# First batch's keys pooled for both partition halves at once, normalising shared between two engines, and another order of the start

## The chip, the cores and the metric

The kernel runs on one core of one Trainium2 chip. The time is device time of one execution in microseconds (us). A core has a matrix engine (PE, which takes its stationary operand by a weight load, PEld, and writes into PSUM), a vector engine (DVE), an activation engine (ACT), GpSimd (POOL) and a queue processor (SP). Each works through its own instructions in order and meets the others at semaphores. In this kernel POOL issues nearly all input loads, and SP issues the stores and DMA transposes.

## The reference

Attention with pooled keys and values, followed by a mixer of two small networks, over 8 batches of 8 heads, 576 rows and head width 64. All inputs and the output are fp32.

```python
k_p = k.reshape(B, H, 72, 8, D).mean(axis=3)          # 576 rows pooled by 8
v_p = v.reshape(B, H, 72, 8, D).mean(axis=3)
scores = q @ k_p.T / sqrt(D);  attn = softmax(scores) # 576 x 72 per head
x = (attn @ v_p) laid out as [B, 576, 512]
u = x + (relu(x.T @ w_tok1) @ w_tok2).T               # token mix: 576 -> 256 -> 576
out = u + relu(u @ w_ch1) @ w_ch2                     # channel mix: 512 -> 1536 -> 512
```

## The kernel before

Each batch has a main part of 512 rows, four interleaved groups of 128 called j = 0 to 3, and a tail of 64 rows. A unit (class `Unit`) handles two groups of one batch: unit a has groups 0 and 1, unit c groups 2 and 3, and `TailUnit` t the tail. Units of batch 1 are a1, c1, t1, and of batch 2 a2, c2, t2. The names below are those of the code.

Attention of a unit goes like this. `qT` (L367) turns q on PE, `copy_qT` (L374) brings it to SBUF. `S(i)` (L382) computes scores against `kbd`, the pooled keys of a head in block-diagonal form: a [128, heads, 2, 72] tile in which the partitions 0 to 63 hold the keys for the first group of rows and the partitions 64 to 127 hold the same keys again for the second. So every pooled head must be copied twice, to two partition halves. The score index i stands for heads 0-2, 3-5 (432 columns of scores) and 6-7 (288 columns). `shift(i)` (L391) takes the row maximum on DVE. It has two forms. The plain one subtracts the maximum on DVE (L398, L400), and `do_E` then needs one exponential on ACT (L416). The "biased" one only takes the negated maximum (L395), and `do_E` (L404) runs one ACT activation of 72 columns per head and group, with the maximum as its bias (L413). `PT` (L424) turns the probabilities on PE, `copy_PT` (L430) copies them, `AV` (L439 to L457) multiplies by the pooled values `vpx` and sums the probabilities, and `norm` (`norm_first`, L459) divides on DVE by a reciprocal and one multiply over all eight heads.

Batch 0's keys are pooled in two halves of four heads (`pool_half`, L299), since they are loaded in two halves: heads 0-3 by SP as fp32, cast on DVE, and heads 4-7 by POOL. The pooling is a product with a banded matrix `pool_m` on PE. It makes two PSUM tiles per half: even heads land in the partitions 0 to 63, odd heads in 64 to 127. `copy_half` (L314) copies each into `kbd`, two copies of 64 partitions x 144 columns per call, four calls in all.

The token mix takes steps (`A_step`, L636, one per row group and a last one for the tail), a relu (`act_A`, L652, on ACT for half 0 and DVE for half 1), the second product and residual (`u`, L655; `add_u`, L664, on ACT for odd j and DVE for even j), and turns the result (`turn_u`, `copy_uT`, L670 and L675) for the channel mix. The channel mix (`c_stream`, from L1004) has for batch 0 three column blocks in which it starts with half of the rows (L1049), then wide blocks (L1017), then the second product (L1033), which uses `wc2` in three parts.

The order of the instructions is the order in which the functions are called; no scheduler changes it. `begin` (L764) holds two lists written by hand. The first (L771 to L861) covers batch 0's attention and token mix and is emitted as it stands. The second, from L863, covers batch 1's attention and token mix and the first steps of batch 2. It is woven with batch 0's `c_stream` by `weave` (L29), which takes from the one or the other so that the shares of the costs (the first argument of `add`) advance together. `fill` (L727), `warm` and the counts given to `S` and `AV` (`keep_running`, L256) add matmuls on a zero tile `idle` whose result is not used. From batch 2 on the streams are built by other functions.

Loads are issued on POOL in the order of the calls before `begin` (L1082 to L1094): `load_w_tok` (L233: w1m, w1t, w2r), `load(1, ...)` (L117: k, q of batch 1), the three parts of `w_ch1` and `w_ch2` (L245, L250), and among them `clear_probs` (L222), one memset on POOL that zeroes the unused columns of the probability tiles, and `split_w_tok2` (L241), two POOL copies.

Of the kernel before, what the change touches and what calls it, by code (L numbers as in the profile page):

```python
# [48 lines left out]
def kernel(  # L49
# [249 lines left out]
    def pool_half(hf):  # L299

        km, kt = main_t[0][0], tail_t[0][0]
        kp = [ps.tile([P, 2, SP], FP32, name="pa") for _ in range(2)]
        for i in range(2):
            for j in range(NJ):
                for hl in range(2):
                    nc.tensor.matmul(out=kp[hl][hl * D:(hl + 1) * D, i, 0:SPM], lhsT=km[:, 4 * hf + 2 * i + hl, j, :],
                                     rhs=pool_m[:, 0:SPM], start=(j == 0), stop=(j == NJ - 1))
        for i in range(2):
            for hl in range(2):
                nc.tensor.matmul(out=kp[hl][hl * D:(hl + 1) * D, i, SPM:SP], lhsT=kt[:, 4 * hf + 2 * i + hl, :],  # L310
                                 rhs=pool_t[0][:, SPM:SP], start=True, stop=True)
        half_ps[hf] = kp

    def copy_half(hf, hl, copy):  # L314
        heads = kbd[0].rearrange("p (r t) e n -> p r t e n", t=2)[:, 2 * hf:2 * hf + 2]
        src = half_ps[hf][hl][hl * D:(hl + 1) * D]
        copy(out=heads[0:D, :, hl, 0, :], in_=src)
        copy(out=heads[D:P, :, hl, 1, :], in_=src)
# [40 lines left out]
    class Unit:  # L359
# [82 lines left out]
        def norm(self, e):  # L442
            norm_first(*self.ao[e])
# [15 lines left out]
    def norm_first(xo, rows, ao, sums):  # L459
        den = sm_pool.tile([P, H], FP32, name="den")  # L460
        nc.vector.reciprocal(out=den[rows], in_=sums[rows])
        nc.vector.tensor_tensor(out=xo[rows].rearrange("p (h d) -> p h d", d=D), in0=ao[rows],
                                in1=den[rows, :, None].broadcast_to([rows.stop - rows.start, H, D]), op=ALU.mult)
# [23 lines left out]
    class TailUnit:  # L487
# [39 lines left out]
        def shift(self):  # L527
            self.sh = []
            for s in self.sc:
                mx = sm_pool.tile([P, 8], FP32, name="mx")  # L530
                nc.vector.tensor_reduce(out=mx[:, 0:HP], in_=s, axis=AX.X, op=ALU.max)
                sh = sh_pool.tile([P, 6, SP], FP32, name="sh")
                nc.vector.tensor_tensor(out=sh[:, 0:HP], in0=s, in1=mx[:, 0:HP, None].broadcast_to([P, HP, SP]),
                                        op=ALU.subtract)
                self.sh.append(sh)

        def do_E(self):
            self.probs = prob_t[self.g % 2]
            for i, sh in enumerate(self.sh):
                nc.scalar.activation(out=self.probs[:, i, :, 0:SP], in_=sh[:, 0:HP], func=AF.Exp)  # L540
# [48 lines left out]
        def norm(self):  # L589
            norm_first(*self.ao)  # L590
# [173 lines left out]
    def begin():  # L764
# [6 lines left out]
        add(0, fill, 11)  # L771
        add(0, fill, 16)
        add(0, pool_half, 0)
        add(0, c.qT, 0, HP)
        add(0, copy_half, 0, 1, nc.scalar.copy)
        add(0, pool_half, 1)
        add(0, copy_half, 0, 0, nc.scalar.copy)
        add(0, a.qT, 0, HP)
        add(0, c.qT, HP, H)
        add(0, c.copy_qT, 0, HP, nc.scalar.copy)  # L780
        add(0, a.qT, HP, H)
        add(0, a.copy_qT, 0, HP, nc.vector.tensor_copy)
        add(0, c.S, 0, 1)
        add(0, copy_half, 1, 1, nc.vector.tensor_copy)
        add(0, a.S, 0)
        add(0, c.shift, 0, True)
        add(0, copy_half, 1, 0, nc.scalar.copy)
        add(0, a.shift, 0, True)
        add(0, c.copy_qT, HP, H, nc.vector.tensor_copy)
        add(0, a.copy_qT, HP, H, nc.scalar.copy)  # L790
        add(0, a.S, 1, 1)
        add(0, a.S, 2, 1)
        add(0, c.do_E, 0)
        add(0, warm, 7)
        add(0, a.shift, 1, True)
        add(0, t.turn_q)
        add(0, c.S, 2)
        add(0, a.shift, 2, False)
        add(0, a.do_E, 0)
        add(0, c.shift, 2, False)  # L800
        add(0, c.S, 1, 1)
        add(0, a.do_E, 2)
        add(0, t.copy_qT)
        add(0, pool_v, 0)
        add(0, a.do_E, 1)
        add(0, a.PT, 0)
        add(0, a.PT, 1)
        add(0, c.do_E, 2)
        add(0, c.shift, 1, False)
        add(0, copy_v, 0)  # L810
        add(0, a.copy_PT, 0, nc.vector.tensor_copy)
        add(0, c.do_E, 1)
        add(0, t.S)
        add(0, a.copy_PT, 1, nc.scalar.copy)
        add(0, a.AV, 0, 1)
        add(0, t.shift)
        add(0, a.norm, 0)
        add(0, t.do_E)
        add(0, c.PT, 0)
        add(0, c.copy_PT, 0, nc.scalar.copy)  # L820
        add(0, a.AV, 1, 1)
        add(0, c.PT, 1)
        add(0, a.norm, 1)
        add(0, c.AV, 0, 1)
        add(0, t.PT)
        add(0, c.norm, 0)
        add(0, c.copy_PT, 1, nc.scalar.copy)
        add(0, c.AV, 1, 1)
        add(0, t.copy_PT, nc.scalar.copy)
        add(0, m0.A_step, (0,))  # L830
        add(0, t.AV)
        add(0, c.norm, 1)
        add(0, m0.A_step, (1,))
        add(0, m0.A_step, (3,))
        add(0, t.norm)
        add(0, m0.A_step, (2,))
        add(0, m0.A_step, (4,))
        add(0, m0.act_A, 0)
        add(0, m0.act_A, 1)
        add(0, a1.qT)  # L840
        add(900, a1.copy_qT, 0, H, nc.scalar.copy)
        add(0, m0.u, 2)
        add(0, m0.add_u, 2)
        add(0, m0.u, 1)
        add(0, m0.u, 0)
        add(0, m0.u, 3)
        add(0, m0.add_u, 1)
        add(0, m0.add_u, 0)
        add(0, m0.turn_u, 1)
        add(0, m0.turn_u, 0)  # L850
        add(0, sum_k, 1)
        add(0, m0.turn_u, 2)
        add(0, m0.add_u, 3)
        add(0, m0.copy_uT, 2, nc.scalar.copy)
        add(0, m0.copy_uT, 1, nc.vector.tensor_copy)
        add(0, m0.copy_uT, 0, nc.vector.tensor_copy)
        add(0, m0.turn_u, 3)
        add(0, m0.copy_uT, 3, nc.scalar.copy)
        add(0, copy_k, 1, 0)
        add(1170, copy_k, 1, 1)  # L860
        weave(Stream(), st)  # L861
        a2, c2, t2 = units(2)
        st = Stream()  # L863
        add = adder(st)
        add(0, a1.S, 0)
        add(0, c1.qT)
        add(0, t1.turn_q)
        add(0, load, 3, (2,))
        add(848, a1.shift, 0)
        add(0, a1.S, 1)  # L870
        add(1170, c1.copy_qT, 0, H, nc.vector.tensor_copy)
        add(0, c1.S, 0)
        add(0, a1.S, 2)
        add(530, a1.shift, 1)
        add(0, a1.do_E, 1)
        add(212, a1.shift, 2)
        add(1060, c1.shift, 0)
        add(0, c1.S, 1)
        add(1378, c1.shift, 1)
        add(0, a1.do_E, 0)  # L880
        add(0, c1.S, 2)
        add(0, a1.do_E, 2)
        add(0, pool_v, 1)
        add(0, a1.PT, 0)
        add(0, c1.do_E, 0)
        add(212, c1.shift, 2)
        add(1800, t1.copy_qT)
        add(0, c1.do_E, 1)
        add(0, t1.S)
        add(910, a1.copy_PT, 0, nc.vector.tensor_copy)  # L890
        add(0, c1.do_E, 2)
        add(0, load_v, 3, 0, 2)
        add(0, sum_v, 2)
        add(1060, t1.shift)
        add(540, copy_v, 1)
        add(0, c1.PT, 0)
        add(0, t1.do_E)
        add(0, a1.PT, 1)
        add(560, a1.copy_PT, 1, nc.scalar.copy)
        add(1400, c1.copy_PT, 0, nc.vector.tensor_copy)  # L900
        add(0, c1.PT, 1)
        add(1150, a1.do_AV, 0)
        add(0, t1.PT)
        add(1400, t1.copy_PT, nc.vector.tensor_copy)
        add(1150, t1.do_AV)
        add(910, c1.copy_PT, 1, nc.scalar.copy)
        add(1150, c1.do_AV, 0)
        add(0, c2.qT)
        add(920, c1.do_AV, 1)
        add(0, sum_k, 2)  # L910
        add(0, t2.turn_q)
# [225 lines left out]
```

## Time and profile before

| what | us or share |
|---|---|
| three timed runs | 279.21, 279.45, 279.54 (median 279.45) |
| the profiled execution | 279.35, of which the span from first to last instruction is 277.3 |
| PE busy | 269.7 (97%), 2174 matmuls |
| DVE, ACT, POOL busy | 164.0 (59%), 121.6 (44%), 116.2 (42%) |
| mean granted PE clock | 0.998 |
| DMA | 42.27 MB, mean 152 GB/s; q0, the loads that POOL issues, 17.93 MB |

A line of the timeline gives the start in the span, the time from the start of the first to the end of the last of a run of equal instructions, the engine, the source line, the operation, output<-inputs, shapes and count. In square brackets stands the idle time of that engine just before, and what ended it. A later instruction of an engine can start before the earlier one's recorded end, so costs in a row are taken from start to start. In a DMA issue line the last number is the time from issue to landing.

### The profile page before, as it was taken

The page shows a single profiled execution, that of the slowest core. Times are in us where ns is not written, and L with a number is a line of the kernel's source. Part 1 is how long each engine was busy: PE and PEld are TensorE (multiplying, and loading weights), DVE is VectorE, ACT ScalarE, POOL GpSimd, SP SyncE. Part 2 cuts the span into 40 slices and gives each one's busy share as a digit, 9 for nine tenths or more (in the row PEclk, how much of TensorE's full clock was granted, in tenths as well). Part 3 has the DMA queues.
Part 4 walks back from the last instruction along what each step waited for, and adds up shares of the span by engine and source line. Part 5 has one row for each costly group of instructions (what it writes and reads, how often), then busy time and mean ns, then how long its engine had stood idle before and what let it go on. Part 6 is the DMA issues. An engine that isn't in the chain of part 4 may idle for free.

```text
span 277.3 us, 5510 instructions
## 1 busy us (share of the span) xinstructions
PE 269.7 (97%) x2174; PEld 145.2 (52%) x2174; DVE 164.0 (59%) x379; ACT 121.6 (44%) x237; POOL 116.2 (42%) x159
## 2 busy tenths in 40 slices
PE   6799999999999999999999999999999999999994
PEld 4565856554445454474545544475544454554463
DVE  6386686688659852694479662775479452520112
ACT  6595587415533463045534552054623550036220
POOL 8699234785529868183459264920000000000000
PEclk9999999999999999999999999999999999999999
DMA  8999999996999999989997999658366701461013
GB/s 141 183 195 203 200 199 200 194 209 145 200 136 188 214 274 158 215 149 162 168 193 155 209 197 193 156 143 137 82 84 156 178 2 39 113 97 38 38 40 113
DMA packets 98969, 42.27 MB, mean 152 GB/s; under 512 B 68800, under 2 KB 94400, under 8 KB 98944
## 3 DMA queue, kind: packets, MB, share of 16 engines
q0 software_dynamic: 35616, 17.93, 49.6%
q1 hardware_dynamic: 63184, 23.93, 41.8%
q8 instruction: 17, 0.28, 0.4%
q10 hardware_dynamic: 144, 0.07, 0.1%
q14 instruction: 8, 0.07, 0.1%
HBM read 35.85 MB, written 9.44 MB: 163 GB/s over the span
## 4 chain that ended last, share of the span: by engine, by line
PE 90%; DVE 3%; DMA 2%; ACT 2%; POOL 1%; issue 1%; POOLq 0%
PE pa L1033 34%; PE pa L1017 31%; PE pa L682 4%; PE pa L478 3%; PE pa L388 3%; DMA qm<-in_q_dram 2%; PE pa L607 2%; PE pt L428 1%; ACT probs L413 1%; PE pa L661 1%; PE pa L625 1%; PE pt L625 1%; DVE xm L483 1%; PE pa L1049 1%; PE pt L372 1%; PE pa L645 1%
## 5 line engine op out<-in xcount | busy, mean ns | idle before, releaser
L1033 PE MATMUL pa<-wc,GT 128*128 128x512 bf16 (+2 forms) x444 | 104.1, 374 | 0.0
L1017 PE MATMUL pa<-uTm,wc 128*128 128x512 bf16 x372 | 89.6, 379 | 0.0
L1019 ACT ACTIVATE GT<-pa 128x512 bf16<-128x512 f32 x105 | 62.1, 597 | 62.5 <-PE pa L1017 62.2
L1017 PEld LDWEIGHTS <-wc 128*128 128x128 bf16 x564 | 44.8, 97 | 36.2 <-issue 1.2
L1033 PEld LDWEIGHTS <-GT 128*128 128x128 bf16 x444 | 41.0, 98 | 42.1 <-issue 1.2
L416 ACT ACTIVATE probs<-sh 128x432 bf16<-128x432 f32 (+1 forms) x45 | 22.9, 524 | 56.8 <-DVE sh L400 56.8
L1037 DVE TENSOR_TENSOR o<-pa,um 128x512 f32<-128x512 f32 (+2 forms) x33 | 22.1, 671 | 28.2 <-PE pa L1033 28.0
L355 POOL TENSOR_TENSOR s<-vs 72x512 f32<-72x512 bf16 x24 | 27.6, 1149 | 15.8 <-DMA vs<-in_v_dram 14.3
L400 DVE TENSOR_TENSOR sh<-pa,mx 128x432 f32<-128x432 f32 (+1 forms) x45 | 24.9, 554 | 3.8
L398 DVE TENSOR_REDUCE mx<-pa 128x6 f32<-128x432 f32 (+1 forms) x45 | 24.6, 546 | 3.2 <-PE pa L388 3.0
L483 DVE TENSOR_TENSOR xm<-pa,den 128x256 bf16<-128x256 f32 x56 | 23.8, 424 | 1.9
L482 DVE RECIPROCAL den<-pa 128x4 f32<-128x4 f32 x60 | 10.6, 177 | 18.6 <-PE pa L478 18.4
L1065 POOL DMA_DIRECT2D out_dram<-o x1 | 0.6, 620 | 49.2 <-DVE o L1037 49.2
L683 DVE TENSOR_TENSOR um<-pa,xm 128x512 bf16<-128x512 f32 x24 | 16.1, 688 | 5.6 <-PE pa L682 5.4
L356 POOL TENSOR_TENSOR s<-s 72x256 f32<-72x256 f32 x24 | 17.3, 722 | 1.9
L388 PE MATMUL pa<-kbd,qT 128*128 128x144 bf16 x128 | 15.4, 226 | 0.5 <-ACT qT L376 0.5
L388 PEld LDWEIGHTS <-qT 128*128 128x128 bf16 x128 | 10.7, 98 | 9.2 <-ACT qT L376 1.1
L478 PEld LDWEIGHTS <-pT 72*128 72x128 bf16 (+1 forms) x256 | 11.5, 99 | 6.8 <-issue 0.8
L682 PE MATMUL pa<-AT,w2m 128*128 128x512 bf16 x48 | 13.8, 379 | 0.0
L478 PE MATMUL pa<-vpx,pT 72*128 72x65 bf16 (+1 forms) x256 | 12.8, 194 | 0.0
L259 PE MATMUL pa<-idle 128*128 128x288 bf16 (+2 forms) x42 | 10.2, 389 | 2.2 <-DVE idle L168 2.2
L603 DVE TENSOR_SCALAR AT<-pa 128x512 bf16<-128x512 f32 x6 | 4.2, 692 | 13.1 <-PE pa L611 7.3
(150 smaller groups left out, 284.7 us busy)
## 6 DMA issues: line engine op xcount, KB each, us to landing
out_dram<-o SPq DMA_DIRECT2D x30, 256.0 KB, 2.5
vs<-in_v_dram POOLq DMA_DIRECT2D x7, 512.0 KB, 10.8
km<-in_k_dram POOLq DMA_DIRECT2D x7, 512.0 KB, 9.3
qm<-in_q_dram POOLq DMA_DIRECT2D x7, 512.0 KB, 12.1
wc<-in_moe_w_ch_dram POOLq DMA_DIRECT2D x6, 512.0 KB, 11.8
out_dram<-o SPq DMA_DIRECT2D x8, 128.0 KB, 2.4
o<-in_k_dram SPq DMA_DIRECT2D x2, 256.0 KB, 2.9
qm<-in_q_dram POOLq DMA_DIRECT2D x2, 256.0 KB, 6.1
```

The lines of the kernel that those rows point to most:

```text
L355: nc.gpsimd.tensor_tensor(out=s4, in0=vs[:, hs, 0:4], in1=vs[:, hs, 4:8], op=add)
L388: nc.tensor.matmul(out=sc[:, (h - h0) * 2:(h - h0) * 2 + 2, :], lhsT=qTs[self.b][:, 2 * h + self.jj, :], rhs=kbd[self.b % NB][:, h], start ...
L398: nc.vector.tensor_reduce(out=mx[:, 0:n], in_=sc, axis=AX.X, op=ALU.max)
L400: nc.vector.tensor_tensor(out=sh[:, 0:n], in0=sc, in1=mx[:, 0:n, None].broadcast_to([P, n, SP]), op=ALU.subtract)
L416: nc.scalar.activation(out=self.probs[:, :, h0:h1, 0:SP].rearrange("p e h n -> p h e n"), in_=self.sh[i][:, 0:(h1 - h0) * 2].rearrange("p ...
L478: nc.tensor.matmul(out=ao[r, hh, :], lhsT=probs_of(h, r), rhs=vpx[b % NB][:, h, :], start=True, stop=True)
L483: nc.vector.tensor_tensor(out=xo[rows, hf * HP * D:(hf + 1) * HP * D].rearrange("p (h d) -> p h d", d=D), in0=ao[rows, :, 0:D], in1=den[ro ...
L682: nc.tensor.matmul(out=u_ps, lhsT=w2m[:, m, j, :], rhs=ATs[b][:, m, :], start=(m == 0), stop=(m == 1))
L1017: nc.tensor.matmul(out=g_ps[:, i, :], lhsT=wc1[:, kk, m * P:(m + 1) * P], rhs=uTs(kk, 0, width), start=(kk == 0), stop=(kk == 3))
L1019: nc.scalar.activation(out=GT[:, m0:m0 + per, :], in_=g_ps, func=AF.Relu)
L1033: nc.tensor.matmul(out=hold["ps"], lhsT=GT[:, kk, j * P:(j + 1) * P], rhs=wc2[:, kk, cols], start=(kk == 0), stop=(kk == NM - 1))
L1037: nc.vector.tensor_tensor(out=o_sb, in0=hold["ps"], in1=us(j)[:, cols], op=ALU.add)
```

## The change

`pool_half` makes one PSUM tile per half with all four heads and computes each head twice, into the partitions 0 to 63 and 64 to 127: 40 matmuls for 20. `copy_half` is then one copy of 64 partitions x 288 columns (all four heads) per call, with the partition half as its argument. There are four copies in all for eight; DVE does those of the upper partition half, ACT those of the lower.

`norm` takes a flag `shared`: DVE multiplies five heads, and ACT scales the other three with one activation of 64 columns each. Only c's second group uses it. The tail unit's `shift` and `do_E` get the biased form. Which groups are biased changes: before, c's 0 and a's 0 and 1; after, c's 0 and 2 and the tail.

The first list is reordered: a's scores start before q's second half is turned for c, c's second q copy goes to ACT, a's second pT copy goes from ACT to DVE, the tail's `AV` goes ahead of the second `A_step`, and 22 fillers stand ahead of the pooling for 27. The second list has another order and other weights. On POOL, `clear_probs` goes ahead of all of these loads, and the third part of `w_ch1`, batch 1's v and `split_w_tok2` change places with others.

```diff
     def pool_half(hf):
 
         km, kt = main_t[0][0], tail_t[0][0]
-        kp = [ps.tile([P, 2, SP], FP32, name="pa") for _ in range(2)]
-        for i in range(2):
+        kp = ps.tile([P, HP, SP], FP32, name="pa")
+        for i in range(HP):
             for j in range(NJ):
-                for hl in range(2):
-                    nc.tensor.matmul(out=kp[hl][hl * D:(hl + 1) * D, i, 0:SPM], lhsT=km[:, 4 * hf + 2 * i + hl, j, :],
-                                     rhs=pool_m[:, 0:SPM], start=(j == 0), stop=(j == NJ - 1))
...
+                for rows in half:
+                    nc.tensor.matmul(out=kp[rows, i, 0:SPM], lhsT=km[:, HP * hf + i, j, :], rhs=pool_m[:, 0:SPM],
+                                     start=(j == 0), stop=(j == NJ - 1))
...
-    def copy_half(hf, hl, copy):
-        heads = kbd[0].rearrange("p (r t) e n -> p r t e n", t=2)[:, 2 * hf:2 * hf + 2]
-        src = half_ps[hf][hl][hl * D:(hl + 1) * D]
-        copy(out=heads[0:D, :, hl, 0, :], in_=src)
-        copy(out=heads[D:P, :, hl, 1, :], in_=src)
+    def copy_half(hf, e, copy):
+        rows = slice(e * D, (e + 1) * D)
+        copy(out=kbd[0][rows, HP * hf:HP * hf + HP, e, :], in_=half_ps[hf][rows])
...
+    def norm_first(xo, rows, ao, sums, shared=False):
         den = sm_pool.tile([P, H], FP32, name="den")
         nc.vector.reciprocal(out=den[rows], in_=sums[rows])
+        hv = H - 3 if shared else H
+        nc.vector.tensor_tensor(out=xo[rows, 0:hv * D].rearrange("p (h d) -> p h d", d=D), in0=ao[rows, 0:hv],
+                                in1=den[rows, 0:hv, None].broadcast_to([rows.stop - rows.start, hv, D]), op=ALU.mult)
+        for h in range(hv, H):
+            nc.scalar.activation(out=xo[rows, h * D:(h + 1) * D], in_=ao[rows, h, :], func=AF.Copy,
+                                 scale=den[rows, h:h + 1])
...
     # TailUnit.shift(biased), TailUnit.do_E: as Unit's
+                if biased:
+                    nc.vector.tensor_reduce(out=mx[:, 0:HP], in_=s, axis=AX.X, op=ALU.max, negate=True)
+                    self.sh.append((s, mx))
+                    continue
...
+                    for h in range(HP):
+                        nc.scalar.activation(out=self.probs[:, i, h, 0:SP], in_=sh[0][:, h, :], func=AF.Exp,
+                                             bias=sh[1][:, h:h + 1])
```

The first list after the change, to the end of the attention:

```python
fill 16, fill 6, pool_half 0, copy_half(0, 1, DVE), a.qT(0, 4), c.qT(0, 4), c.copy_qT(0, 4, DVE),
copy_half(0, 0, ACT), pool_half 1, copy_half(1, 1, DVE), a.copy_qT(0, 4, ACT), a.S(0, 1 filler), a.qT(4, 8),
c.S(0, 1), copy_half(1, 0, ACT), a.copy_qT(4, 8, DVE), c.shift(0, biased), a.S(1, 1), c.qT(4, 8), a.shift(1),
warm 9, c.copy_qT(4, 8, ACT), c.do_E 0, a.shift(0), a.S 2, c.S(1, 1), a.do_E 0, t.turn_q, t.copy_qT, a.shift(2),
c.S(2, 1), a.do_E 1, pool_v, a.do_E 2, c.shift(2, biased), c.do_E 2, c.shift(1), a.PT 0, copy_v,
a.copy_PT(0, DVE), a.PT 1, t.S, a.AV 0, c.do_E 1, c.PT 0, t.shift(biased), a.copy_PT(1, DVE), t.do_E,
a.AV(1, 1), c.copy_PT(0, ACT), a.norm 0, c.PT 1, a.norm 1, c.copy_PT(1, ACT), t.PT, c.AV 0, A_step 0, c.norm 0,
c.AV 1, t.copy_PT, t.AV(1), A_step 2, A_step 1, c.norm(1, shared), t.norm, A_step 3, A_step 4
```

On POOL:

```diff
+    clear_probs()
     load_w_tok()
     load(1, (0, 1))
     load_w_ch1(0)
-    clear_probs()
+    load_w_ch1(2)
     load_w_ch1(1)
+    load(1, (2,))
+    split_w_tok2()
     load_w_ch2(0)
-    load(1, (2,))
-    load_w_ch1(2)
-    split_w_tok2()
     load_w_ch2(1)
     load(2, (1, 0, 2))
     load_w_ch2(2)
```

More of the change, by code (lines that the diff above doesn't have):

```diff
@@ L525, in S, with shift @@
             self.sc = sc
[L527 removed]
+        def shift(self, biased=False):
             self.sh = []
@@ L836, in begin @@
-        add(0, m0.A_step, (2,))
         add(0, m0.A_step, (4,))
-        add(0, m0.act_A, 0)
         add(0, m0.act_A, 1)
         add(0, a1.qT)
-        add(900, a1.copy_qT, 0, H, nc.scalar.copy)
+        add(0, m0.act_A, 0)
+        add(0, m0.u, 0)
+        add(0, m0.add_u, 0)
+        add(180, a1.copy_qT, 0, H, nc.scalar.copy)
         add(0, m0.u, 2)
-        add(0, m0.add_u, 2)
         add(0, m0.u, 1)
-        add(0, m0.u, 0)
         add(0, m0.u, 3)
         add(0, m0.add_u, 1)
-        add(0, m0.add_u, 0)
+        add(0, m0.turn_u, 0)
@@ L935, in begin @@
+        add(690, m1.add_u, 2)
+        add(0, m1.uT, 2, 2)
+        add(0, copy_k, 2, 0)
+        add(1800, t2.copy_qT)
         return st
```

217 lines of the change are left out of this document (107 added, 110 removed).

## The prediction

> **What bounds the kernel now.** I read the page's busy table and its chain of waits first, then the stretches before the steady part, then the timelines of ACT, DVE, PE and POOL and the DMA issues there.
>
> ```profile
> PE 269.7 (97%) x2174; PEld 145.2 (52%) x2174; DVE 164.0 (59%) x379; ACT 121.6 (44%) x237; POOL 116.2 (42%) x159
> ...
> PE 90%; DVE 3%; DMA 2%; ACT 2%; POOL 1%; issue 1%; POOLq 0%
> ```
>
> Over the whole span PE is the bound; the chain leaves it for a tenth. Where it leaves it is seen in a table of stretches (engine busy times, granted clock, DMA share, GB/s):
>
> ```profile
> 10.54:12.96 2.42, 1.88 (x21) 1.25 (x22) 1.69 (x5) 1.61 (x4) 0.93 (x1) 1.00 1.72 185
> 12.96:22.33 9.37, 9.16 (x139) 6.35 (x137) 8.15 (x18) 9.36 (x28) 8.89 (x8) 1.00 1.46 195
> 22.33:29.83 7.50, 7.48 (x103) 4.45 (x100) 5.02 (x11) 2.80 (x5) 5.67 (x9) 1.00 1.26 207
> 29.83:61.80 31.97, 31.97 (x312) 19.60 (x310) 23.99 (x56) 18.45 (x35) 17.81 (x25) 1.00 1.43 203
> ```
>
> From 29.83, where batch 0's channel mix begins (L1049), PE is busy 31.97 of 31.97: what arrives earlier there ends earlier, and what DVE or ACT do there is covered. From 12.96 to 22.33 ACT is busy 9.36 of 9.37: batch 0's exponentials and copies set that stretch. PE's 9.16 there are no bound, since they contain 7 fillers in a row and single ones (L259, matmuls whose result is not used). Before 10.54 the loads set the pace:
>
> ```profile
> 9.23 0.44 PE L306 MATMUL pa<-pool_m,km 128*64 128x64 bf16 x16 [0.56 <-DMA km<-in_k_dram]
> ...
> 10.54 0.62 PE L372 MATMUL pt<-ident,qm 128*128 128x128 bf16 x8 [0.50 <-DMA qm<-in_q_dram]
> ```
>
> So the change can act on three pieces: from 10.54 to ACT's first exponential, ACT's stretch, and the token mix to 29.83.
>
> **Pooling and its copies.** 40 matmuls a half for 20. The 16 L306 of a half begin at 9.23 and the next line at 9.50 follows: 0.27/16, about 0.017 each in pairs of column halves, so 20 more cost 0.31 or so. Half 0 runs before km's second half lands (9.15), half 1 before q's second half lands (10.54), and five fillers fewer (22 for 27; 27 take 5.75 from 2.17 on, 0.21 each) come ahead: nothing on the path. Without that cover it would be 2x0.31. The copies: eight at 0.27 to 0.31 become four of 64x288, whose rows exist at L333 (DVE 0.46, ACT 0.39-0.40). Both read one tile now, and ACT's waits for DVE's. The second half's pair is done near 11.0, when the first scores can start; before, the last of them was DVE's at 11.98+0.31.
>
> **To the first exponential.**
>
> ```profile
> 11.20 0.42 DVE L376 COPY qT<-pt 128x512 bf16<-128x512 bf16 x1 [4.69 <-PE pt L372]
> 11.65 0.31 DVE L317 CAST kbd<-pa 64x144 bf16<-64x144 f32 x1
> 11.98 0.31 DVE L318 CAST kbd<-pa 64x144 bf16<-64x144 f32 x1
> 12.32 1.12 DVE L395 TENSOR_REDUCE mx<-pa 128x6 f32<-128x432 f32 x2
> ```
>
> DVE does two small copies behind the last q copy and ahead of the first maximum. Both are gone from that place, and c's scores no longer need q's second half: its first maximum can start near 11.34, 0.98 earlier. ACT gains less, as c's second q copy now lies ahead of the exponentials: it starts near 11.99 (PE turns c's second half after a's and two score matmuls) and takes 0.48 to the next start. First exponential 12.47 for 12.96: -0.5.
>
> **ACT's stretch.**
>
> ```profile
> 12.96 2.64 ACT L413 ACTIVATE probs<-pa,mx 128x72 bf16<-128x72 f32 x12 [0.34 <-DVE mx L395]
> ...
> 15.99 1.48 ACT L413 ACTIVATE probs<-pa,mx 128x72 bf16<-128x72 f32 x6
> ...
> 19.81 1.92 ACT L431 COPY pT<-pt 72x1024 bf16<-72x1024 bf16 x2
> ```
>
> A biased group costs ACT an activation per head; from start to start 0.205 (15.99 to 17.22 for six). One unbiased activation of 432 columns takes 0.45 (18.03 to 18.48), one of 288 columns 0.33, but costs DVE a subtract (0.52 or 0.37). Before: 18x0.205 + 0.45 + 3x0.34 + vpx 0.48 + q-tail copy 0.25 + three pT copies (0.98, 0.92, 0.94) and the tail's 0.58 make 9.3, which is the stretch. After: biased are c0 (6), c2 (4), t (4), so 14x0.205; a0, a1, c1 unbiased 3x0.45; a2 0.33; 0.25; 0.48; two pT copies 1.8; 0.58. That is 7.66, or 1.64 less. Given back: DVE, which gets two subtracts of 432 and one pT copy (0.60) and loses two of 288, works through c0's maximum, a1, a0, a2, c2, c1 from 11.34 with no pause, so a0's subtract ends near 14.25 while ACT is through c0 at 13.70: 0.55 of waiting; t's maximum is late too, 0.2, and the last pT 0.2. ACT's last copy ends at 12.47+7.66+0.95, near 21.1, for 22.33: -1.2, of which -0.5 came in with the first exponential. If DVE's chain is as slow as its longest rows (0.60 for the reduce, 0.61 for the subtract: +0.09 each over four pairs) 0.5 is lost; if ACT never waits, 0.95 is gained.
>
> **Shared normalising.** c's second group: DVE's multiply goes from 512 columns (0.61) to 320 (about 0.42 in proportion); ACT does three of 64 columns. The nearest rows are L413's 72 columns, 0.205 each, so 0.6 on an ACT that has ended its copies. ACT ends after DVE by some 0.2 to 0.4, but x_tail's multiply, last before the token mix's tail step, comes 0.19 earlier. I take 0, with 0.2 either way. The new order of steps, tail last, then lets the token mix (PE 7.48 busy of 7.50) begin 1.2 earlier and keep all but 0.2 at its ACT and DVE hand-overs (idle PE is some tenths at 24.7 to 29.8, and act_A, add_u only change engine order): L1049 near 28.85 for 29.83, -1.0.
>
> **Batch 1 woven in.** The matmuls are the same ones in another order; PE has no gap there to fill and none to spare. A wait that the new order opens shows as a gap, a saved one as nothing: 0.1 either way for none seen, up to +0.3.
>
> **The moved memset and loads.** POOL issues the loads, and a memset stands between them:
>
> ```profile
> 7.88 0.60 POOL L236 DMA_DIRECT2D w1m<-in_moe_w_tok_dram  x1
> ...
> 13.44 0.69 POOL L142 DMA_DIRECT2D kt<-in_k_dram  x1 [1.73 <-DMA vs<-in_v_dram]
> ...
> 16.41 3.88 POOL L223 MEMSET probs<- 128x4480 bf16 x1
> ```
>
> Its 3.77 (16.41 to 20.18) now come at 7.88: w1m, both w1t, w2r, and batch 1's k issue from 11.65, 3.3 to 3.8 later. Against that, POOL waited 0.51 and 1.73 for landings before the old place, which the memset now fills, so q of batch 1 goes out 1.6 later and the second wc chunk 2 earlier. What matters is whether the DMA engines go empty. At 7.88 they have v and the q tail ahead of them, to 14.1 (issue 7.21 plus 6.9). A load of 512 KB, km at 161.2, landed after 6.7 on a quiet queue; at 200 GB/s 2.6 of that is transfer, so data begins some 4.1 after issue: 15.75 for a 256 KB w1m with half of that transfer still to come, at worst, where its landing was 15.3. I take a slip d of 0 to 0.45 for the stream. The slowest quiet row (vs at 72.47, 384 KB in 8.8) allows 4.5 for w1m's slip. The loads keep their total, so the last one of this phase to be late counts:
>
> ```profile
> wc<-in_moe_w_ch_dram POOLq DMA_DIRECT2D x1, 512.0 KB, 13.2
> ```
>
> This is w_ch2's third part, issued at 37.85, landed 51.05, first used by L1033 at 52.83: 1.78 of slack. With PE 1.0 earlier and d to 0.45 it still holds. Batch 1's q (issued 14.11, 9.1 to landing, needed at about 24) has 0.6. The new order of the w_ch1 chunks puts the one needed last in third place, at about 31.3 for a need after 33.
>
> A rule of the Trainium skill speaks against the moved memset: by its page "SBUF — State Buffer", section "Who interferes with whom", VectorE's second port pair is GpSimd's and is taken as an exclusive lock, and the loser waits. This is a rival below, priced there by rows.
>
> **Sum.** The profiled run took 279.35, span 277.3 and 2.05 around it, 0.1 under the median 279.45. First exponential -0.5, ACT's stretch -0.7, lost in the token mix +0.2, woven part and shared multiply 0, loads 0, rounded: -1.1 from 279.35 is 278.25, and with the median's 0.1, 278.3. Own range 277.8 to 278.8 (DVE's chain +0.5, ACT's waits -0.5).
>
> **Rivals.**
> 1. A late load gives the gain back. It decides from d over 0.6 (batch 1's q) or 0.7 (w_ch2's third part, 1.78-1.1). For it: w1m alone slips 3.8 at issue. Against: the two waits that absorb it, and PE can go on with channel mix. Half to all of the 1.1 is lost: 278.8 to 279.4.
> 2. The stream starves by the whole 3.77 of POOL. It decides from d over 1.78: 279.35+3.77-1.78 = 281.3. For it the 8.8 of vs; against it km's 6.7, and loads queued to 14.1.
> 3. The memset holds up DVE from 7.9 to 11.65, just where four copies and the first maximum now lie: if these wait to 11.65, two kbd copies (0.46), two q copies (0.33) put the maximum at 13.2, 0.9 after the old one: 279.45+0.8 = 280.3. Against it: pT's copy ran inside the old memset in 0.69 (17.71) and outside, at 39.37, in 0.68. The Trainium skill has the reason in "VectorE: DVE Perf Modes", section "Why PSUM operands drop a tier": an operand in PSUM never uses the second port; the trace agrees.
> 4. DVE is the bound of the stretch, nearly as long as ACT was: its 8.15 busy plus 2x0.52+0.60-2x0.37 is 9.05, less copies that come earlier. Then ACT's 1.64 counts for nothing, only the earlier maximum's 0.98 less 0.3: 278.8.
> 5. ACT hardly waits, 0.95 more: 277.4.
>
> **How the numbers follow.** Forecast with case 4's near end 0.63; case 1 0.20; case 5 0.08; case 2 0.06; case 3 0.03. No more than 0.2% (0.56) either way cannot be told from no change: all of 278.9 to 280.0. From case 1 most of 0.20 less 0.06, plus 0.02 of the rest: same 0.16; slower 0.09 from cases 2, 3; faster 0.75. Range 277.7 to 279.3: the low end half of case 5, the high end nearly all of case 1.
>
> **What would show it.** Right: the first L395 at 11.3, first L413 near 12.5, ACT's last pT copy near 21.1, first L1049 near 28.8, PE without gaps after. Wrong: 64x288 copies beyond 0.46 or ending after 11.2 (case 3); w1m landing beyond 17, or PE idle behind a DMA at 24, 33 or 52 (1, 2); DVE busy and ACT waiting over 1.5 from 12 to 21 (4); L1049 early but the end not, with PE gaps behind DVE or ACT between 30 and 62: the woven order.

## The result: slower, and the profile after

The changed kernel takes 283.76 us (median of four runs, 283.03 to 284.05) against 279.44 (279.21 to 279.54) for the kernel before: a ratio of 1.015, 95% interval 1.0129 to 1.0172. The prediction said 278.3. The profiled execution took 283.62, span 281.6, which is 4.3 more than the span before.

The page's busy table and chain of the changed kernel:

```profile
PE 267.7 (95%) x2182; PEld 146.6 (52%) x2210; DVE 169.5 (60%) x379; ACT 120.7 (43%) x232; POOL 116.1 (41%) x159
...
PE 85%; DVE 8%; DMA 2%; POOL 1%; issue 1%; ACT 1%; DVEq 0%; POOLq 0%
```

PE's busy time is 2.0 less than before, it covers 85% of the chain, not 90%, and DVE 8% where it had 3%. DVE's busy time is 5.5 more with the same 379 instructions, so some DVE instruction has become long. The table of stretches tells where PE stood (engine busy times in the order PE, PEld, DVE, ACT, POOL, then granted clock, DMA share, GB/s):

```profile
0.00:10.54 10.54, 4.88 (x54) 3.37 (x55) 8.30 (x17) 4.68 (x10) 9.34 (x18) 1.00 1.03 152
10.54:12.96 2.42, 1.11 (x16) 1.06 (x15) 1.88 (x3) 0.20 (x1) 2.42 (x4) 0.77 1.60 166
12.96:22.33 9.37, 9.23 (x127) 6.48 (x126) 7.44 (x16) 6.30 (x20) 7.39 (x10) 0.88 1.20 147
```

ACT has 0.20 of work from 10.54 to 12.96 where it had 1.61. Everything is late before ACT's stretch begins. The timeline of the changed kernel, POOL's line first, then DVE, PE, ACT and PE again:

```profile
7.88 3.88 POOL L223 MEMSET probs<- 128x4480 bf16 x1
...
5.71 6.28 DVE L189 COPY pool_t<-diag 64x8 bf16<-64x8 bf16 x2 [0.24 <-POOL diag L184]
...
11.85 0.33 PE L310 MATMUL pa<-pool_t,kt 128*64 128x8 bf16 x7 [4.79 <-DVE pool_t L189]
...
17.14 1.38 ACT L411 ACTIVATE probs<-pa,mx 128x72 bf16<-128x72 f32 x6
...
33.10 1.91 PE L1060 MATMUL pa<-uTm,wc 128*128 128x256 bf16 x16
...
75.92 0.43 PE L480 MATMUL pa<-vpx,pT 72*128 72x65 bf16 x8 [1.22 <-DMA pT<-probs]
```

And the same DVE line in the kernel before:

```profile
5.71 0.80 DVE L189 COPY pool_t<-diag 64x8 bf16<-64x8 bf16 x2 [0.24 <-POOL diag L184]
```

Two copies of 64x8 elements, which make the pooling matrix for the tails (`pool_t`, L186 to L190, in code that the change does not touch), went from 0.80 to 6.28 us together: the first took 6.08 for 0.16, the second 0.17 for 0.61. The first ends at 11.79, when POOL's memset ends (7.88 + 3.88 = 11.76). PE needs `pool_t` for the last matmuls of each pooled half (L310), so it stood for 4.79 behind 32 matmuls that were done. The first biased exponential comes at 17.14 for 12.96, the channel mix at 33.10 for 29.83: 3.27 later. The rest of the 4.3 is a second place, PE's wait of 1.22 at 75.92 for the transposed probabilities of batch 2; the kernel before has no wait over 0.2 after 17.32.

### The profile page after: what moved, and what is told of

Read it like the earlier page. It is cut to its first block, busy times and chain, and to the rows that moved or that the text cites. A ratio compares the mean times of both kernels' runs of the same rounds, so it can differ in the third digit from the quotient of the medians.

```text
span 281.6 us, 5553 instructions
## 1 busy us (share of the span) xinstructions
PE 267.7 (95%) x2182; PEld 146.6 (52%) x2210; DVE 169.5 (60%) x379; ACT 120.7 (43%) x232; POOL 116.1 (41%) x159
## 4 chain that ended last, share of the span: by engine, by line
PE 85%; DVE 8%; DMA 2%; POOL 1%; issue 1%; ACT 1%; DVEq 0%; POOLq 0%
PE pa L1044 31%; PE pa L1028 30%; PE pa L693 3%; PE pa L480 3%; PE pa L386 2%; DVE pool_t L189 2%; DVE sh L398 2%; PE pa L618 2%; DMA pT<-probs 2%; DVE mx L396 2%; PE pa L672 1%; PE pa L636 1%; PE pt L636 1%; PE pt L370 1%; PE pa L1060 1%
## 5 line engine op out<-in xcount | busy, mean ns | idle before, releaser
L1044 PE MATMUL pa<-wc,GT 128*128 128x512 bf16 (+2 forms) x426 | 101.7, 373 | 1.1 <-issue 0.3
L353 POOL TENSOR_TENSOR s<-vs 72x512 f32<-72x512 bf16 x24 | 27.6, 1149 | 14.8 <-DMA vs<-in_v_dram 13.4
L398 DVE TENSOR_TENSOR sh<-pa,mx 128x432 f32<-128x432 f32 (+1 forms) x46 | 25.7, 559 | 3.9
L396 DVE TENSOR_REDUCE mx<-pa 128x6 f32<-128x432 f32 (+1 forms) x46 | 25.3, 551 | 3.1 <-ACT GT L1063 1.5
L693 PE MATMUL pa<-AT,w2m 128*128 128x512 bf16 x45 | 13.1, 379 | 0.0
L267 POOL COPY kk<-km 128x1024 bf16<-128x1024 bf16 x8 | 8.1, 1036 | 10.9 <-DMA km<-in_k_dram 8.4
```

The costliest lines, as they stand in the source:

```text
L353: nc.gpsimd.tensor_tensor(out=s4, in0=vs[:, hs, 0:4], in1=vs[:, hs, 4:8], op=add)
L396: nc.vector.tensor_reduce(out=mx[:, 0:n], in_=sc, axis=AX.X, op=ALU.max)
L398: nc.vector.tensor_tensor(out=sh[:, 0:n], in0=sc, in1=mx[:, 0:n, None].broadcast_to([P, n, SP]), op=ALU.subtract)
L693: nc.tensor.matmul(out=u_ps, lhsT=w2m[:, m, j, :], rhs=ATs[b][:, m, :], start=(m == 0), stop=(m == 1))
L1044: nc.tensor.matmul(out=hold["ps"], lhsT=GT[:, kk, j * P:(j + 1) * P], rhs=wc2[:, kk, cols], start=(kk == 0), stop=(kk == NM - 1))
```

## The experiments

Fifteen kernels. "Ratio" is against the kernel before that was timed with it, with its 95% interval where there is one. "Start" is the first biased exponential, "mix" the first matmul of the channel mix, "wait" PE's wait for `pT` between 70 and 76, in the profiled execution as "start" and "mix" are.

| kernel | median, before beside it | ratio | start | mix | wait |
|---|---|---|---|---|---|
| before | 279.44 | | 12.96 | 29.83 | none |
| changed | 283.76 | 1.015 (1.0129 to 1.0172) | 17.14 | 33.10 | 1.22 |
| e1 memset in its old place | 278.81 / 279.23 | 0.9983 (0.9969 to 0.9998) | 12.43 | 28.90 | 1.30 |
| e2 before, memset first | 282.89 / 279.23 | 1.0129 (1.011 to 1.0149) | 16.47 | 33.36 | none |
| e3 pool_t copied by ACT | 281.13 / 279.23 | 1.007 (1.0049 to 1.0092) | 12.31 | 29.96 | 1.34 |
| e4 memset four issues later | 279.98 / 279.23 | 1.0024 (1.0008 to 1.0041) | 12.58 | 30.42 | none |
| e5 e1, old second list | 278.41 / 279.59 | 0.9949 (0.9929 to 0.9968) | 12.61 | 28.57 | none |
| e6 before, new pooling alone | 280.32 / 279.59 | 1.0026 (1.0014 to 1.0038) | 12.35 | 29.88 | 1.23 |
| e7 memset in four pieces | 283.31, one run | | 17.90 | 33.85 | none |
| e8 pool_t by tensor_tensor | 281.50, one run | | 12.91 | 30.11 | none |
| e9 memset one issue later | 284.56, one run | | 18.55 | 35.10 | none |
| e10 memset near 39 us | 278.85 / 279.36 | 0.9977 (0.9963 to 0.9991) | 12.98 | 28.94 | none |
| e11 e10, norm not shared | 278.71 / 279.36 | 0.9977 (0.9961 to 0.9993) | 12.20 | 28.74 | 1.44 |
| e12 before, 36 more matmuls | 280.18 / 279.36 | 1.0024 (1.0005 to 1.0042) | 13.13 | 30.02 | 1.25 |
| e13 memset three issues later | 280.47, one run | | 12.64 | 29.42 | none |
| e14 e10, 36 more matmuls | 278.17 / 279.23 | 0.9957 (0.994 to 0.9974) | 12.14 | 28.35 | none |
| e15 e10, old second list | 278.65 / 279.23 | 0.9977 (0.9959 to 0.9995) | 12.79 | 28.75 | none |

"Start" has to be read beside the landing of k's second half, which moves by some tenths from one execution to another: PE begins the second pooling at 9.23 in before, at 9.09 in e1, 9.28 in e5, 9.63 in e10, 8.76 in e14.

### Is it the memset, and what does it hold?

e1 puts the memset back in the changed kernel; e2 moves it, and nothing else, in the kernel before.

```diff
 e1, against the changed kernel            e2, against the kernel before
-    clear_probs()                         +    clear_probs()
     load_w_tok()                               load_w_tok()
     load(1, (0, 1))                            load(1, (0, 1))
     load_w_ch1(0)                              load_w_ch1(0)
+    clear_probs()                         -    clear_probs()
```

> The changed kernel with the POOL memset of the probability tiles put back behind w_ch1's first part, all else as changed. Theory L (the memset, recorded from 7.88 to 11.76, holds DVE's 64x8 copy of pool_t, which took 6.08 us instead of 0.61, and with it the pooling): the copy takes about 0.6 again, the first biased exponential starts near 12.5 instead of 17.14, the first matmul of the channel mix near 28.9 instead of 33.10. The end is then 278.3 if nothing else is wrong with the prediction, and about 279.4 if PE's 1.22 us wait at 75.92 for the turned probabilities of batch 2 belongs to the new second list (theory W) and stays. Rival P (the doubled pooling or the new copies cost the time): first exponential stays beyond 15, the end over 281.

> The kernel before, with only the memset moved ahead of the late loads. Theory L: DVE's copy of pool_t again takes about 6.1 us, PE waits nearly 5 us for it, the first exponential comes 4 to 5 us later than 12.96, and the end is 283 to 284. Rival P: the memset alone does little, the end is 279.2 to 280.

e1's first exponential is at 12.43 and its channel mix begins at 28.90; theory L holds and P falls. The time is 278.81, between the two that were named, and its ten runs form two groups, 277.98 to 278.49 and 279.13 to 279.47; the profiled one belongs to the upper. Its PE timeline:

```profile
24.64 0.39 PE L672 MATMUL pa<-AT,w2m 128*128 128x512 bf16 x1 [0.22 <-POOL w2m L243]
25.22 0.82 PE L672 MATMUL pa<-AT,w2m 128*128 128x512 bf16 x3 [0.19 <-POOL w2m L243]
...
71.81 0.43 PE L480 MATMUL pa<-vpx,pT 72*128 72x65 bf16 x8 [1.30 <-DMA pT<-probs]
```

PE is now early enough to wait for POOL's split of w_tok2, 0.41 in all, and in this execution the wait for `pT` takes the gain back. e2 is 3.66 us slower than before, with its first exponential 3.5 later (4 to 5 were expected), and its two copies again take 6.28 together, so the new pooling is not needed for the loss.

e3 lets ACT make `pool_t`, e8 keeps DVE but uses an addition of two SBUF tiles, e7 cuts the memset in four.

```diff
-        nc.vector.tensor_copy(out=pool_t[s][half[s], SPM:SP], in_=diag[...])
+        nc.scalar.copy(out=pool_t[s][half[s], SPM:SP], in_=diag[...])                   # e3
+        nc.vector.tensor_tensor(out=pool_t[s][half[s], SPM:SP],                         # e8
+                                in0=pool_t[s][half[s], SPM:SP], in1=diag[...], op=ALU.add)
...
-        nc.gpsimd.memset(prob_all.rearrange("p t e h n -> p (t e h) n")[:, :, SP:P], 0.0)
+        cols = prob_all.rearrange("p t e h n -> p (t e h) n")                           # e7
+        for c in range(SP, P, 14):
+            nc.gpsimd.memset(cols[:, :, c:c + 14], 0.0)
```

> The changed kernel, memset in front, with the two 64x8 copies of pool_t done by ACT instead of DVE, so that DVE has no copy from SBUF to SBUF left there. If the memset only holds DVE's operation between SBUF tiles (theory L, narrow): the two kbd copies of DVE run at about 0.46 inside the memset, the first exponential is near 12.5, the end 278.3 (279.4 with theory W). If it holds every DVE operation (theory L, wide): DVE's first kbd copy does not end before 11.7, the first exponential comes at 15 or later, the end over 281. If POOL's loads being 3.8 us later is what costs, the end stays over 280 with an early first exponential and PE waits on DMA.

> The changed kernel, memset in front, with DVE's two 64x8 copies of pool_t made as additions of diag to the zeroed tile (tensor_tensor with both inputs in SBUF). If every DVE operation between SBUF tiles is held by the memset, the first addition takes about 6 us and the end is 283.6. If it is the copy's form that is held, the additions take under 0.7 together and the end is that of e3, about 281.1. The Trainium skill (page SBUF - State Buffer, section Who interferes with whom) says the second: a DVE instruction with two SBUF inputs is held only by a GpSimd instruction that reads SBUF, and a memset only writes.

> The changed kernel, memset in front, made by four memsets of 14 columns each (about 0.97 us apiece) that follow each other. If DVE's copy of pool_t is held for one instruction of POOL at a time (L, each), it ends when the first piece ends, near 8.9 or earlier, and the end is that of e3, about 281.1. If it is held as long as POOL has such work without a break (L, whole), it ends near 11.8 as in the changed kernel, and the end is 283.6.

In e3 and e8 the memset still runs from 8.01 and 7.91 for 3.88, and inside it DVE copies `kbd` out of PSUM in 0.46, as outside. e8's two additions take 0.34 together:

```profile
5.73 0.34 DVE L189 TENSOR_TENSOR pool_t<-pool_t,diag 64x8 bf16<-64x8 bf16 x2 [0.25 <-POOL diag L184]
```

So neither DVE as such nor all its work between SBUF tiles is held, only the copy. This is what the Trainium skill says on its page "SBUF — State Buffer", section "Who interferes with whom": a copy between SBUF tiles can take the port pair that VectorE shares with GpSimd, and a two-input operation is held only by a GpSimd instruction that reads SBUF. The traces agree on who is held and who is not; the ports themselves are in no trace. In e7 the copy ends at 12.28, with the last of four memsets (8.26 + 4.00 = 12.26): it does not get in between them.

But e3 and e8 are not fast. e3's PE timeline and its row of the stretch that had 195 GB/s before:

```profile
25.62 0.62 PE L370 MATMUL pt<-ident,qm 128*128 128x128 bf16 x8 [1.92 <-DMA qm<-in_q_dram]
...
53.97 1.02 PE L1044 MATMUL pa<-wc,GT 128*128 128x512 bf16 x4 [1.02 <-DMA wc<-in_moe_w_ch_dram]
```

```profile
12.96:22.33 9.37, 8.91 (x151) 6.86 (x151) 8.41 (x20) 7.82 (x24) 7.52 (x10) 1.00 1.15 139
```

The loads are late. Batch 1's q, issued at 15.69, lands 9.9 later, at 25.6 for 23.2; w_ch2's third part lands at 53.9 (40.49 + 13.4) for 51.05. The stretch moved 56 GB/s less for 9.37 us (e1, with the memset in its old place, moved 196), that is 0.52 MB, which at 200 GB/s is an estimated 2.6 us of transfer. In the changed kernel none of this shows, since PE itself is over 3 us late.

### From where does the hold begin?

The copy started 2.17 ahead of the memset and yet lost to it. e4, e9 and e13 move the memset behind all four, one and three issues of `load_w_tok`.

> The changed kernel with the memset four DMA issues later, behind load_w_tok, at about 10.3 to 14.2. Theory L, narrow: the copy of pool_t takes about 0.6, DVE's copies and maxima out of PSUM run inside the memset at their usual times, the end within 0.4 of e1's. Theory L, wide: DVE stands from 10.3 to 14.2, the first exponential is near 16, the end over 281.

> The changed kernel with the memset one DMA issue later, behind w1m, at about 8.4 to 12.3. The copy of pool_t starts at 5.71, 2.2 us ahead of the memset's recorded start in the changed kernel, and was held all the same; with four issues between (e4) it was not. If the hold begins with the memset's own time on POOL and the copy merely failed to get in before it, one more issue of 0.55 us changes nothing: the copy takes over 6 us, PE waits 5 us for it, the end is 283.6. If POOL's next work decides when the copy is let in, it is free at about 6.3 as before, and the end is that of e3 and e8, 280.7 to 281.5.

> The changed kernel with the memset three DMA issues later, behind w2r, at about 9.7 to 13.6. In e9 (one later) the copy of pool_t, started at 5.71, was held 6.64 us, to 12.35; in e4 (four later) it was not held. If the hold reaches back a fixed time of some 2.7 us from the memset's start, the copy is free near 6.3 here. If it reaches back by instructions, it is free only from four on: held to 13.6, PE waits over 6 us, the end near 285.

The DVE and POOL timelines of e9:

```profile
5.71 6.84 DVE L189 COPY pool_t<-diag 64x8 bf16<-64x8 bf16 x2 [0.24 <-POOL diag L184]
```

```profile
8.44 3.89 POOL L223 MEMSET probs<- 128x4480 bf16 x1
```

and of e13:

```profile
5.71 0.80 DVE L189 COPY pool_t<-diag 64x8 bf16<-64x8 bf16 x2 [0.24 <-POOL diag L184]
```

```profile
9.68 3.90 POOL L223 MEMSET probs<- 128x4480 bf16 x1
```

A memset recorded 2.73 after the copy's start holds it, one recorded 3.97 after does not (nor e4's at 10.20). In before the first of the two copies is done at 5.87 (5.71 and 0.16), and up to there POOL's recorded instructions are the same in all these kernels, so the hold reaches back at least 2.0 us ahead of the memset's recorded start in the changed kernel and 2.6 in e9. In e13 the second copy is done 3.2 ahead of it. Whether what decides is a time between the two or a number of instructions in POOL's queue (the memset was the fourth and fifth behind `diag` where it held, the seventh and eighth where it did not) stays open. In e4 DVE's maxima and subtracts ran inside the memset at their usual 0.60 and 0.61; e4 and e13 lose by loads instead (PE waits 1.18 and 0.93 for batch 1's q, e13 another 0.95 for w_ch2), so e4 is not within 0.4 of e1, as theory L had it, but 1.2 above.

### The second wait, at 70 to 76

e5 and e15 use the second list as it was; e6 puts only `pool_half` and `copy_half` into the kernel before.

> The kernel of e1 (memset in its old place) with the second list of begin as it was before the change. Theory W (PE's wait of 1.30 us at 71.81 in e1 for batch 2's turned probabilities belongs to the new second list): no wait over 0.4 on PE between 60 and 80, the first channel-mix matmul at 28.9 as in e1, and this 0.9 is kept to the end: 278.3. Rival W2 (the wait comes with any list once PE starts 0.9 earlier, since the chain of batch 2 over DVE, ACT and SP does not): a wait of 0.9 or more stays, the end at 279.2, as before.

> The kernel before with only pool_half and copy_half as changed (40 matmuls a half, one copy of 64x288 per call), in the old order. If the four copies are what they cost elsewhere (DVE 0.46, ACT 0.39), the last kbd copy on DVE ends 0.1 to 0.2 earlier than 12.29, the first maximum and the first exponential with it, and the end is 0.1 to 0.3 lower: 279.0. If the doubled matmuls are on the path (theory P), the first exponential is 0.2 to 0.6 later than 12.96 and the end 279.5 to 279.9.

e5 came out as theory W had it, 278.41 and no wait. But e6, which has the old list, waits 1.23 at 72.79 (and at 280.32 ends above both of its forecasts), and e8, which has the new one, does not: W falls. What goes with the wait is a packet of instructions on the queue q8. Every trace has 17 of them:

```profile
q8 instruction: 17, 0.28, 0.4%
```

The sixth comes between 69 and 78 (in e14 near 63), and in every trace a hole in the transfers follows it. The half microseconds of before and of the changed kernel (last column GB/s; the packet is in 74.00 and in 73.00):

```profile
74.00:74.50 0.50, 0.41 (x2) 0.10 (x1) 0.47 (x2) 0.40 (x1) 0.50 (x1) 1.00 1.71 211
74.50:75.00 0.50, 0.44 (x3) 0.20 (x3) 0.01 (x1) 0.00 (x0) 0.50 (x2) 1.00 0.16 16
75.00:75.50 0.50, 0.50 (x4) 0.26 (x3) 0.00 (x0) 0.31 (x1) 0.50 (x2) 1.00 0.30 41
```

```profile
73.00:73.50 0.50, 0.50 (x5) 0.25 (x4) 0.47 (x3) 0.28 (x1) 0.00 (x0) 1.00 1.10 193
...
74.00:74.50 0.50, 0.50 (x4) 0.10 (x1) 0.49 (x2) 0.23 (x1) 0.00 (x0) 1.00 3.76 44
74.50:75.00 0.50, 0.20 (x1) 0.00 (x0) 0.43 (x3) 0.26 (x1) 0.00 (x0) 1.00 0.04 3
75.00:75.50 0.50, 0.00 (x0) 0.00 (x0) 0.37 (x2) 0.34 (x1) 0.00 (x0) 1.00 0.09 10
```

In before the last transpose of c2's probabilities had landed by then, and a later transpose of q takes the hole. In the changed kernel a transpose of c2's, issued at 70.88, lands in 5.0 where the same one took 3.3 in before (issued at 67.69), and PE goes empty. All 17 traces fit this. Where the sixth packet comes 2.4 to 3.1 us after that transpose is issued (changed, e1, e3, e6, e11, e12), the transpose lands in 5.0 to 5.2 and PE waits 1.22 to 1.44. Where it comes 3.8 us or more after (e2, e4, e5, e7 to e10, e13, e15 and before), or ahead of it (e14), it lands in 3.2 to 3.3 and PE does not wait. Up to the half microsecond of the packet PE had 729 weight loads in before and 729 in the changed kernel, 730 in e1 and e3, and 739 to 748 in e5, e6, e8 and e10, so it seems to come by PE's place in its own instructions. The change adds 36 matmuls (2210 weight loads for 2174), most of them in the pooling, and so brings the packet forward against the rest of the work. e12 tests this in the kernel before, e14 moves the packet once more.

```diff
-        add(0, fill, 11)                                                    # e12, in the kernel before
+        add(0, lambda: keep_running(ps.tile([P, D], FP32, name="pa"), 47))
...
-        add(0, fill, 6)                                                     # e14, in e10
+        add(0, lambda: keep_running(ps.tile([P, D], FP32, name="pa"), 42))
```

> The kernel before with its first 11 fillers of 288 columns replaced by 47 of 64 columns: 36 matmuls more, as the change has, at no later a time. In every trace so far a packet of instructions (queue q8) is fetched when PE has had 729 to 748 weight loads, and for about 1.5 us behind it the DMA engines move next to nothing. Theory F (the 36 additional matmuls bring this fetch forward by as many instructions, into the last transposes of batch 2's probabilities): the packet comes near 70.5 instead of 74, PE waits 1.0 to 1.3 us for pT near 72.8, and the end is 280.3, as with e6. If the fetch does not go by PE's count, or the wait is something else in the change, the end stays at 279.2 to 279.6.

> The kernel of e10 with 6 fillers of 288 columns replaced by 42 of 64 columns: 36 matmuls more again, with no later pooling. Theory F: the instruction packet comes another 3 to 4 us earlier, near 66.5 to 67, and its hole falls ahead of or on the first of c2's two transposes; PE's wait at 72 is then there in nearly all runs if the hole pushes the transposes along (end 279.5 to 280), or in none if they are issued behind it (278.6). If the fetch does not go by PE's count, it stays at 70.5 and the runs spread as in e10, 278.85.

e12's PE timeline:

```profile
72.94 0.43 PE L478 MATMUL pa<-vpx,pT 72*128 72x65 bf16 x8 [1.25 <-DMA pT<-probs]
```

Theory F holds in e12. The packet comes in the half microsecond from 70.0, after 729 weight loads, PE waits 1.25, and the median goes from 279.36 to 280.18; the twelve runs again split, 279.13 to 279.38 and 280.05 to 281.02, as they would if the packet sometimes misses the transpose, though only one of them was profiled. In e14 the packet comes near 63, some 3.5 earlier than was expected, after 728 weight loads. Its hole (58, 7 and 47 GB/s) meets a2's transposes (issued at 61.3 and 62.6, landed in 4.4 and 3.9), for which PE does not wait, and none of c2, and the wait is gone: 278.17, 0.9957 of before.

A packet by itself makes no hole. In before, the 1.5 us behind the first, the fourth, the fifth and the sixth of them, and a hole that has no packet in it:

```profile
15.42:16.92 1.50, 1.46 (x13) 0.79 (x10) 1.43 (x4) 1.50 (x8) 1.50 (x3) 1.00 1.37 197
46.82:48.32 1.50, 1.50 (x32) 1.12 (x30) 1.40 (x6) 0.81 (x2) 0.28 (x1) 1.00 1.21 195
57.17:58.67 1.50, 1.50 (x13) 0.91 (x12) 1.32 (x3) 0.00 (x0) 1.42 (x2) 1.00 1.34 249
74.49:75.99 1.50, 1.43 (x7) 0.68 (x7) 0.02 (x1) 0.60 (x1) 1.50 (x4) 1.00 0.60 75
...
77.50:78.00 0.50, 0.50 (x11) 0.30 (x9) 0.32 (x1) 0.01 (x1) 0.00 (x0) 1.00 0.21 9
```

That the place of the sixth packet decides about this wait is shown by e12 and by the 17 traces; what stops the DMA engines behind it, and not behind the first five, is not shown.

### The other parts

> The changed kernel with the memset behind w_ch2's third part, near 40 us, where POOL waits for landings anyway and nothing needs the cleared columns before 60. No copy held, no load late before 40, and the waits for w2m (0.41 us in e1) gone: first channel-mix matmul at 28.5 to 28.9, the end 278.0. If the 1.3 us hole of the DMA engines between 69 and 75 meets the last transposes of batch 2's probabilities, as in half of e1's runs, 279.1 in those runs.

> The kernel of e10 (memset behind w_ch2's third part) with the second list as before the change, that is, e5 with the memset out of the way too. First channel-mix matmul at 28.5 to 28.9; the end 278.2 to 278.6 if e5's 0.9949 came from the first list alone, below 278.2 if the later memset adds to it.

> The kernel of e10 with c's second normalising on DVE alone. The prediction put the sharing at 0, with 0.2 either way: the first channel-mix matmul within 0.2 of e10's and the end too. If it is worth its three activations, 0.3 or more later.

With the memset near 39 (e10), the waits for w2m are gone and the channel mix begins at 28.94 although k landed 0.4 later than in before; the time, 278.85, is no better than e1's, ratio 0.9977 for 0.9983, where 278.0 was expected. A part of the gain is lost behind the stretch of the table. A later packet comes near 99, 2.5 us behind a transpose of the next batch's probabilities (issued at 96.55), which lands in 4.7; the same one took 3.4 in before (issued at 97.29, with no packet until 106).

```profile
101.28 0.43 PE L480 MATMUL pa<-vpx,pT 72*128 72x65 bf16 x8 [0.25 <-DMA pT<-probs]
```

There e10's lead over the kernel before falls from 0.90 (matmuls of the channel mix at 99.14 for 100.04) to 0.48 (101.55 for 102.03). e4, e5, e8, e13 and e15 have such a wait too, 0.26 to 0.46 between 100 and 104. e14 has none, and its lead of 1.48 at the channel mix (28.35 for 29.83) is still 1.5 at the end (span 275.8 for 277.3).

e15 shows that the old second list adds nothing of its own (0.9977). Its expectation took e5's 0.9949 as a measure of the first list; the two intervals overlap (0.9959 to 0.9995 and 0.9929 to 0.9968), and e5 had only six runs. The shared normalising is worth nothing that these runs can tell: e10 and e11 have the same ratio. From the first exponential to the channel mix e10 takes 15.96 and e11 16.54, but e11 also waited 0.52 for the q tail, so no gain can be read from that.

## Why the prediction was wrong

**What bounds the kernel, and the sign.** The places were right: a loss ahead of the channel mix goes to the end. The forecast was faster with 0.75; it is slower, and by more than any of its cases (281.3 at most). PE's busy time was read only to 61.80; behind that, at 72 and near 101, a transpose that lands late can take back what was gained ahead of it (e1, e10). The sum has a slip besides: -0.5, -0.7 and +0.2 make -1.0, not -1.1.

**The moved memset: the step that failed.** The prediction looked for DVE work between 7.88 and 11.65, the memset's recorded time, and listed four copies and the first maximum, all from PSUM. It left out the copy of `pool_t`, recorded from 5.71 to 6.51, since that lay ahead of the memset. Rival 3, with a chance of 0.03, had the mechanism and the wrong instruction: it priced a maximum 0.9 late and let the row of pT's copy (0.69 inside, 0.68 outside) speak against it. That row is right, and says nothing of a copy whose source and destination are both in SBUF. The held copies ended 5.48 later than before (11.99 for 6.51) and cost 4.20 at the channel mix (33.10 against e1's 28.90).

**The slip d of the loads, mis-sized.** It was taken as 0 to 0.45 from the landing of w1m. w1m did land nearly there (11.78 + 3.7 = 15.5 in e3, for 15.3). The stream behind it slipped by 2.3 to 2.9: after the memset POOL issued k, q and the tails of batch 1 one by one, 0.7 to 1.0 apart, into DMA engines that had run low (90 GB/s from 12 to 14 us in e3, 191 in before). The vs row of 8.8, called quiet there, has the holes at 74.5 and 77.5 in it. So d was past the 1.78 that rival 2 named, and e3 and e8, which show the loads without the held copy, take 281.1 and 281.5 where rival 2 said 281.3.

**To the first exponential, and ACT's stretch: right in the main.** With the memset out of the way, the first exponential comes 3.34, 3.33, 3.35 and 3.38 behind the second pooling in e1, e5, e10 and e14, for 3.73 in before: 0.38 earlier on average, for a forecast of 0.5. From there to the channel mix it is 15.96 in e5, e10 and e15, 16.21 in e14 and 16.47 in e1 (0.41 of it the waits for w2m), for 16.87: 0.4 to 0.9 less, where the forecast was 0.5. Together that is 0.8 to 1.3 for 1.0. The end was forecast at 278.3, and e1, e5, e10, e14 and e15 measure 278.17 to 278.85; of these only e1 and e10 differ from the changed kernel by the memset alone.

**Pooling and copies: right in size, but not free.** e6's first exponential lies 3.66 behind the second pooling, so the pooling by itself is worth 0.07 at the start. Its channel mix begins at 29.88 for 29.83 (k landed 0.5 earlier there, but PE then waited 0.67 for a copy of q and 0.30 for q's tail), so no cost of the matmuls is seen up to there. They still cost 0.7 us in e6 through the packet. **The woven part** was given 0 to +0.3. The wait in it is 1.22 in the changed kernel (about 1.0 more at the end than at the channel mix: 4.3 less 3.27), but by e12, e14, e6 and e8 it goes with PE's count of instructions, not with the new order.

**Shared normalising: 0, as forecast.** The change as a whole thus holds a gain of about 1 us, two losses that stand one behind the other (4.2 by the held copy, which hides the 2.3 by the loads, e3 less e1), and one that comes with the number of matmuls (0.7 and 0.8 in the medians of e6 and e12).

## What to carry to other kernels

Before a long GpSimd instruction is moved, look for every VectorE copy between SBUF tiles near its new place, some microseconds ahead of it as well as inside, and follow who waits for the copy: 64x8 elements stopped PE for 4.8 us. Here an issue queue that was held for 3.8 us did not slip by what its first transfer slipped (0.2 us), but by about what the DMA engines failed to move meanwhile (0.52 MB; the loads came 2.3 to 2.9 late). Work that is hidden on its engine can still shift other events, so when a new wait appears far from a change, test the mere number of instructions by itself.

## What the runs showed of the hardware that was not expected

An instruction recorded as started can be held by one that another engine starts 2.7 us later (e9: 5.71 and 8.44). By the Trainium skill, page "SBUF — State Buffer", section "Who interferes with whom", whoever issues first has the ports; these traces do not agree with that, if the recorded starts are the issues.

The sixth instruction packet stands ahead of 1 to 1.5 us in which 16 DMA engines moved 2 to 58 GB/s (before, changed, e12, e14), and a DMA transpose under way then lands in 5.0 to 5.2 for 3.2 to 3.3. The Trainium skill, page "Runtime: NRT & Kernel Launch", section "Instruction fetch mechanics", calls the cost of crossing from one block of instructions to the next mostly hidden. On PE it was, in the changed kernel (0.50 busy of the 0.50 us with the packet), but not on the transfers that PE waited for next.

After PE's 4.79 us without work its granted clock was half for 3 us in the changed kernel (and from 12 to 15 in e2 and e7 too, where PE had stood for 3.47 and 4.62), a further part of its late start:

```profile
12.00:15.00 3.00, 3.00 (x61) 2.56 (x59) 1.34 (x3) 0.98 (x3) 3.00 (x6) 0.50 1.32 146
```
